# Attention and two mixtures of experts on one core: routing a batch in one piece instead of two halves

## The chip, the cores and the metric

The kernel runs on one core of a Trainium2 chip. The metric is the time of one execution on the device in microseconds (us), median over several runs; less is better. A profiled execution gives a trace of every engine: PE (TensorE, matrix products; PEld are its weight loads), DVE (VectorE), ACT (ScalarE), POOL (GpSimd), SP (SyncE, which issues most DMAs).

## What is computed

Three steps follow each other on 2 batches of 768 tokens with 8 heads of 40 (320 channels).

1. A gated linear attention: a recurrence over time with stabilised gates, per head `C = f*C + i*v k^T`, output `sigmoid(o) * (C q) / max(|n q|, 1)`. The kernel does it in chunks of 128 tokens, 6 per batch, 12 in all.
2. A mixture of 8 experts. Each token goes to the two experts with the largest noisy logits:

```python
logits = x @ w_gate
noise_scale = np.log1p(np.exp(x @ w_noise))
noisy_logits = logits + noise_scale * noise
top2 = np.argpartition(-noisy_logits, 2, axis=1)[:, :2]
top2_w = np.exp(top2_l - max); top2_w /= top2_w.sum() + 1e-09
out[mask] += top2_w[mask, k, None] * (np.maximum(x[mask] @ w1[e], 0) @ w2[e])
```

3. A dense mixture of 4 experts: every token through all four, weighted by normalised given probabilities.

Expert products are done in a split form: each fp32 operand is a high part (fp32r) and a remainder.

## The kernel before

**Attention** (lines 321 to 499, 881). Chunk `i` (0 to 11; 0 to 5 are batch 0) needs some twenty operations, each a small function `o_...`. `attn` is a generator whose every step does one of four pieces (`STEP`, lines 47 to 52) for a running index `i`: piece (i,0) has the state update U(i), the decays D of chunk i+2, the routing logits lg of chunk i-2 (L490, copied by ACT in L491); piece (i,1) has the transposes tp (L455) and the output x (L462 to L468) of chunk i-1, qg of chunk i+1 and the state product inter(i) (L440); piece (i,2) has the decay product G of chunk i+2 (L368); piece (i,3) has S of chunk i+1 (L382), AV(i) (L447), Cu(i) (L426) and the transposes xp of chunk i-1 (L478). So the logits of a batch's last chunk come in piece (7,0) for batch 0 and (13,0) for batch 1. While `alone` is set, a product is preceded by one with zeros (L344).

**Routing** (`route`, line 508; `routed_`, line 593). `route(b, h)` is a generator of ten steps on a half `h` of batch `b` (chunks 0 to 3, or 4 and 5). Step 1: Exp and Ln on ACT, two DVE operations. Step 2: the pairwise comparison `df` and its sum. Step 3: the masks `selb`, `sel`. Step 4: PE counts the tokens ahead of each token (`pp`, L537 and L541). Step 5: eleven small DVE operations on 8 values per chunk (L547 to L558). Step 6: slots and the one-hot matrix `oh` (L570), 256 values per chunk. Step 7: `in_col` and `rh` (L572 to L576). Step 8 is empty. Step 9: PE multiplies `oh` and `rh` into a table (`pt`, L581), DVE adds it; after the second half it is cast to `tok`. Step 10: `back`. `routed_` gives the mixing weights and counts. `tok` is what POOL's indirect DMAs (`xload`, L646) need to gather an expert's tokens; `prep` (L649) transposes and splits those.

**Experts.** `moe1(n)` has 8 steps per unit: four of stage 1 (L207), four of stage 2 (L221). The first four units (experts 0 to 3, batch 0) need only batch 0's routing; unit 4 needs batch 1's. Weights stream in through four `raw` buffers (`w_load`), and ACT and DVE split them (`w_split`, L187 and L188).

**The order.** Two strings set it by hand (lines 36, 37; `follow`, line 982). A group is what stands between two blanks; `A` is the next piece of attention, `r` and `q` a step of the first and the second half's routing, `F` a step of `routed_`, `w` a split of expert 0's first weights with a load, `l` a load, `g` the second sigmoid, `X` the gathers of two units, `P` the first `prep`. PLAN1 runs alone, before the experts; the line that closes `follow` (L997) takes one more piece `A`, so PLAN1 reaches (8,3). PLAN2's groups alternate with the steps of the first four units.

```python
PLAN1 = "A A A A A A A A Al A Ag Al A Al A Al Ar Ar Ar Ar Awr Ar Awr Ar qr Aqr q Aq q Aq q q A qX w A w F A P q F F"
PLAN2 = "AA AA AA AA AA AAr AAr AAr AAr Ar Ar Arq rq rq rq q q q q q q F F F"
```

In PLAN1 the first `r` stands with piece (5,1), the first `q` behind (7,0), the first half's ninth step right behind that `q`. Each engine runs its instructions in a fixed order; on PE it follows the plan.

Of the kernel before, what the change touches and what calls it, by code (L numbers as in the profile page):

```python
# [7 lines left out]
F32 = mybir.dt.float32  # L8
F32R = mybir.dt.float32r
BF16 = mybir.dt.bfloat16  # L10
# [6 lines left out]
P = 128  # L17
B, H, S, D = 2, 8, 768, 40
NC = S // P
# [3 lines left out]
E1, E2, F = 8, 4, 1024  # L23
# [3 lines left out]
NCOL = 4  # L27
# [7 lines left out]

PLAN1 = "A A A A A A A A Al A Ag Al A Al A Al Ar Ar Ar Ar Awr Ar Awr Ar qr Aqr q Aq q Aq q q A qX w A w F A P q F F"
PLAN2 = "AA AA AA AA AA AAr AAr AAr AAr Ar Ar Arq rq rq rq q q q q q q F F F"
RAW = 3 * F // NQ
# [27 lines left out]
def body(ctx: ExitStack, tc: tile.TileContext, d, o, dbg=None):  # L66
    nc = tc.nc
# [5 lines left out]
    at = at_cm.__enter__()  # L73
# [40 lines left out]
    tok = [const.tile([P, E1, NCOL], I32, name=f"tok_{b}") for b in range(B)]  # L114
# [112 lines left out]
    front = {}  # L227
# [71 lines left out]
    def sigmoid(b, after):  # L299
        with tc.issue_after(after):  # L300
            s2 = nc.scalar.activation(xs[b], xs[b], AF.Sigmoid)
        with tc.issue_after(s2.ins):
            front["table"] = nc.scalar.preload_act_table_set("natural_log_exp_and_others").ins
        return front["table"]
# [189 lines left out]
    done = set()  # L494
# [9 lines left out]

    HALVES = (slice(0, 4), slice(4, NC))
    rt = [{}, {}]

    def route(b, h):
        t = rt[b]
        if h == 0:  # L510
            nl = at.tile([P, NC, E1], F32, name="nl")
            selb = at.tile([P, NC, E1], BF16, name="selb")
            sel = at.tile([P, 2, NC, E1], F32, name="sel")
            t.update(nl=nl, selb=selb, sel=sel)
        nl, selb, sel = t["nl"], t["selb"], t["sel"]
        n = HALVES[h]
        c0, HC = n.start, n.stop - n.start
        logit = lgs[b]
        assert ("lg", b * NC + HALVES[h].stop - 1) in done
        sp = at.tile([P, HC, E1], F32, name=f"spl{h}")  # L520
        nc.scalar.activation(sp, logit[:, n, E1:], AF.Exp)
# [3 lines left out]
        yield  # L525
        df = at.tile([P, HC, E1, E1], F32, name=f"df{h}")
        nc.vector.tensor_sub(df, nl[:, n].unsqueeze(2).to_broadcast([P, HC, E1, E1]), nl[:, n].unsqueeze(3).to_broadcast([P, HC, E1, E1]))
        nc.vector.tensor_tensor(df.rearrange("p t a b -> p t (a b)"), df.rearrange("p t a b -> p t (a b)"), thr.rearrange("p a b -> p (a b)").unsqueeze(1).to_broadcast([P, HC, E1 * E1]), ALU.is_ge)
        rk = at.tile([P, HC, E1], F32, name=f"rk{h}")
        nc.vector.tensor_reduce(rk, df, AX.X, ALU.add)  # L530
# [8 lines left out]
        for i in range(1, last + 1):  # L539
            j = max(i, c0)  # L540
            nc.tensor.matmul(pp[:, j - c0 :, :], ones, selb[:, j - i : last + 1 - i, :], start=False, stop=(i == last))  # L541
        sl = at.tile([P, 3, HC, E1], F32, name=f"sl{h}")
        yield
        g = at.tile([P, HC, E1], F32, name=f"g{h}")
        spare = at.tile([P, HC, E1], F32, name=f"spare{h}")
        wide = lambda x: x.unsqueeze(1).to_broadcast([P, HC, E1])
# [12 lines left out]
        yield  # L559
        tmp = at.tile([P, 2, HC, E1], F32, name=f"tmp{h}")  # L560
        sf = at.tile([P, 3, 2, HC], F32, name=f"sf{h}")
        for w in (0, 2):
# [3 lines left out]
        K = 2 * HC  # L566
        oh = at.tile([P, K, P], BF16, name=f"oh{h}")
        rh = at.tile([P, 2, K, E1 * NCOL], BF16, name=f"rh{h}")
        in_col = at.tile([P, K, E1 * NCOL], BF16, name=f"in_col{h}")
        nc.vector.tensor_tensor(oh, count.unsqueeze(1).to_broadcast([P, K, P]), sf[:, 2].rearrange("p k c -> p (k c)").unsqueeze(2).to_broadcast([P, K, P]), ALU.is_equal)  # L570
# [12 lines left out]
        nc.vector.tensor_add(table, table, pt[:, 1])  # L583
        if h == 1:
            nc.vector.tensor_copy(tok[b].rearrange("p e j -> p (e j)"), table)
            routed.add(b)
        yield
# [310 lines left out]
    def fill(n):  # L898

        wps = psum([P, 4 * P], "warm")  # L900
        for i in range(n):
            nc.tensor.matmul(wps, zero[:, :P], zero, start=(i == 0), stop=(i == n - 1))  # L902
# [68 lines left out]
    def splits():  # L971
        for _ in range(NQ):
            with behind():
                w_split()
                w_load()
            yield
# [5 lines left out]
    def follow(plan, b, first):  # L982
        r, q, f, w = route(b, 0), route(b, 1), routed_(b), splits()
        for group in plan.split():
            for t in group:
                if t in "Arqfw":
                    next({"A": A, "r": r, "q": q, "w": w}[t], None)
                elif t == "F":
                    next(f, None)
                elif t == "X":  # L990
                    xload(first)
                    xload(first + 1)
                else:
                    {"l": behind_load, "P": lambda: prep(first), "g": lambda: sigmoid(1, front["act"])}[t]()
            yield
        for g in (A, r, q, f):
            assert next(g, None) is None or g is A  # L997
# [111 lines left out]
```

## Time and profile before

| what | value |
|---|---|
| median of 3 runs | 709.69 us (709.32 to 710.06) |
| profiled execution | 709.88 us, span of its trace 708.1 us |
| PE busy | 690.0 us, 97% of the span |
| DVE, ACT, POOL busy | 370.3, 254.7, 82.1 us |
| mean granted TensorE clock | 0.986 |
| HBM read, written | 64.07 MB, 8.92 MB |

The span is what the trace covers; 1.78 us of the execution lie around it. An engine's share is a mean over stages: attention fills the first 100 us, experts with attention go on to about 130 us, and from there on it is experts almost alone. The granted clock is 1.00 when TensorE runs at 2.4 GHz and 0.50 at 1.2 GHz.

### The profile page before, as it was taken

The numbers are of one execution on the slowest core, as the hardware profiler recorded it, in microseconds if no ns is written. First come the engines' busy times: TensorE is split into PE (matmuls) and PEld (weight loads), VectorE is DVE, ScalarE is ACT, GpSimd is POOL, SyncE is SP. The second block draws the span as 40 slices with busy tenths as digits, with TensorE's granted clock in tenths as the row PEclk, the third lists the DMA queues.
The fourth block names the chain that finished last, engine by engine and source line by source line (L and its number), as shares of the span: only waits on it lengthen the run. The fifth ranks groups of instructions, "written<-read, shape, count | busy, mean of one in ns | idle before, by whom it ended". The sixth has DMA issues, their size and how long they took to land.

```text
span 708.1 us, 11630 instructions
## 1 busy us (share of the span) xinstructions
PE 690.0 (97%) x4612; PEld 616.8 (87%) x4616; DVE 370.3 (52%) x834; ACT 254.7 (36%) x475; POOL 82.1 (12%) x143
## 2 busy tenths in 40 slices
PE   9999789999999999999899999999999999999997
PEld 4566569999999999999889899898998998989987
DVE  7857868797564655658756424412344124332131
ACT  4964236453453543545541313302233013121120
POOL 5211041005012101124024000000000000000000
PEclk9999689999999999999999999999999999999999
DMA  8345446656365454567662003100031001001011
GB/s 276 109 156 181 131 149 184 180 182 219 109 193 164 129 152 127 144 191 243 185 195 82 0 12 101 52 0 1 20 108 37 1 1 38 1 0 38 1 38 40
DMA packets 36434, 73.79 MB, mean 104 GB/s; under 512 B 7576, under 2 KB 14744, under 8 KB 36376
## 3 DMA queue, kind: packets, MB, share of 16 engines
q1 hardware_dynamic: 33752, 64.16, 29.7%
q0 software_dynamic: 2624, 8.85, 4.4%
q8 instruction: 38, 0.62, 0.4%
q14 instruction: 20, 0.16, 0.1%
HBM read 64.07 MB, written 8.92 MB: 103 GB/s over the span
## 4 chain that ended last, share of the span: by engine, by line
PE 87%; DVE 5%; DMA 3%; ACT 2%; issue 2%; POOL 0%; SPq 0%; ACTq 0%; DVEq 0%; POOLq 0%
PE z L207 25%; PE z L221 24%; PE s L207 13%; PE s L221 12%; PE sp L382 2%; PE warm L902 2%; DMA raw<-w 1%; PE s L217 1%; PE hp L440 1%; PE hp L447 1%; DMA raw<-v 1%; PE lp L490 1%; PE pa L660 1%; DVE w1lo L188 1%; PE up L414 1%
## 5 line engine op out<-in xcount | busy, mean ns | idle before, releaser
L224 ACT ACTIVATE hh<-z 128x512 fp32r<-128x512 f32 x96 | 56.9, 598 | 192.7 <-PE z L207 188.8
L221 PE MATMUL z<-w2hi,hh 128*128 128x320 f32 x384 | 118.5, 309 | 0.0
L221 PE MATMUL z<-w2hi,hl 128*128 128x320 f32 x384 | 118.3, 308 | 0.0
L221 PE MATMUL z<-w2lo,hh 128*128 128x320 f32 x384 | 118.3, 308 | 0.0
L207 PE MATMUL z<-x2h,w1hi 128*128 128x512 f32 x288 | 112.4, 390 | 0.0
L221 PE MATMUL s<-w2hi,hh 128*128 128x320 f32 x448 | 108.2, 313 | 2.0 <-ACT hh L224 1.2
L225 DVE SCALAR_TENSOR_TENSOR hl<-z,hh 128x512 fp32r<-128x512 f32 x96 | 65.8, 689 | 82.6 <-ACT hh L224 82.6
L207 PE MATMUL z<-x2h,w1lo 128*128 128x512 f32 x288 | 96.6, 389 | 0.0
L207 PE MATMUL s<-xh,w1hi 128*128 128x256 f32 (+1 forms) x288 | 84.9, 312 | 0.0
L188 DVE TENSOR_TENSOR w2lo<-raw,w2hi 128x640 fp32r<-128x640 f32 x60 | 49.1, 822 | 66.4 <-ACT w2hi L187 64.2
L221 PEld LDWEIGHTS s<-w2hi,hh 128*128 128x128 f32 x448 | 77.0, 188 | 3.1 <-ACT hh L224 1.5
L187 ACT CAST w2hi<-raw 128x640 fp32r<-128x640 f32 x60 | 43.6, 728 | 90.0 <-PE s L217 25.2
L207 PE MATMUL z<-x2l,w1hi 128*128 128x512 f32 x192 | 74.8, 390 | 0.0
L188 DVE TENSOR_TENSOR w1lo<-raw,w1hi 128x768 fp32r<-128x768 f32 x60 | 57.3, 955 | 31.6 <-ACT w1hi L187 30.9
L221 PEld LDWEIGHTS z<-w2lo,hh 128*128 128x128 f32 x384 | 72.1, 188 | 0.6
L221 PEld LDWEIGHTS z<-w2hi,hh 128*128 128x128 f32 x384 | 72.1, 188 | 0.5
L221 PEld LDWEIGHTS z<-w2hi,hl 128*128 128x128 f32 x384 | 72.1, 188 | 0.0
L207 PE MATMUL s<-xh,w1lo 128*128 128x256 f32 (+1 forms) x288 | 70.6, 309 | 0.0
L221 PE MATMUL s<-w2lo,hh 128*128 128x320 f32 x224 | 69.3, 309 | 0.0
L187 ACT CAST w1hi<-raw 128x768 fp32r<-128x768 f32 x60 | 50.1, 836 | 39.7 <-PE s L207 20.2
L207 PEld LDWEIGHTS z<-x2h,w1lo 128*128 128x128 f32 x288 | 54.1, 188 | 11.3
L207 PEld LDWEIGHTS z<-x2h,w1hi 128*128 128x128 f32 x288 | 54.0, 188 | 10.8
(208 smaller groups left out, 994.2 us busy)
## 6 DMA issues: line engine op xcount, KB each, us to landing
raw<-w SPq DMA_DIRECT2D x44, 384.0 KB
raw<-w SPq DMA_DIRECT2D x44, 320.0 KB
raw<-v SPq DMA_DIRECT2D x16, 384.0 KB
raw<-v SPq DMA_DIRECT2D x16, 320.0 KB
kv<-kv SPq DMA_DIRECT2D x12, 324.0 KB
Yd<-ys SPq DMA_DIRECT2D x8, 320.0 KB
kp<-kT SPq DMA_DIRECT2D x12, 208.0 KB
qt<-qT SPq DMA_DIRECT2D x12, 208.0 KB
```

The lines of the kernel that those rows point to most:

```text
L187: nc.scalar.copy(hi, raw)
L188: nc.vector.tensor_sub(lo, raw, hi.bitcast(F32))
L207: nc.tensor.matmul(out_ps, l, r, start=(i == 0), stop=(i == len(seq) - 1))
L217: nc.tensor.matmul(yp, both[f], r[:, k], start=(f == 0 and i == 0), stop=(f == NF - 1 and i == 1))
L221: nc.tensor.matmul(yp, l, r, start=(f == 0 and i == 0), stop=(f == NF - 1 and i == 2))
L224: nc.scalar.activation(hh, src, AF.Relu)
L225: nc.vector.scalar_tensor_tensor(hl, src, 0.0, hh.bitcast(F32), ALU.max, ALU.subtract)
L382: nc.tensor.matmul(sp[g][:, j, :], t["kp"][r, j, :], t["qt"][r, j, :], start=anew, stop=(anew or j == 3))
L414: nc.tensor.matmul(up[64 * j : 64 * j + m, p, :], t["kw"][:, h : h + m], t["kv"][:, 4 * j + p, D:], start=True, stop=True)
L440: nc.tensor.matmul(hp[64 * j : 64 * j + m, p, :], Cs[c % 2][r, 41 * p : 41 * p + m], t["qg"][r, p, :], start=(anew and p == 0), stop=False)
L447: nc.tensor.matmul(hp[64 * j : 64 * j + 41, p, :], t["kv"][:, 4 * j + p, D:], t["A"][:, 4 * j + p, :], start=False, stop=(p == 3))
L902: nc.tensor.matmul(wps, zero[:, :P], zero, start=(i == 0), stop=(i == n - 1))
```

## The change

`route` takes all six chunks of a batch at once: one set of ten steps per batch, each operation on 48 values where it was on 32 and on 16 (the larger ones in proportion). The letter `q` goes, and `o` is new: six products with zeros (`fill(6)`). Both plans are new. In PLAN1 the four `w` stand with pieces (5,1), (5,3), (6,1) and (6,3); no routing is issued before (7,0); the first step follows (7,0), steps 2 and 3 follow (7,1), step 4 follows (7,2), 5 is with (7,3), 6 with (8,0), 7 with (8,1), then 8, `o`, and 9 with `X`. PLAN1 with the closing line reaches (9,0). In PLAN2 the attention has 16 pieces in 11 groups, and the ten steps of batch 1 follow, one per group, in groups 12 to 21.

```diff
-PLAN1 = "A A A A A A A A Al A Ag Al A Al A Al Ar Ar Ar Ar Awr Ar Awr Ar qr Aqr q Aq q Aq q q A qX w A w F A P q F F"
-PLAN2 = "AA AA AA AA AA AAr AAr AAr AAr Ar Ar Arq rq rq rq q q q q q q F F F"
+PLAN1 = "A A A A A A A A Al A Ag Al A Al A Al Aw A Aw A Aw A Aw A r A rr A r Ar Ar Ar r o rX A rF A F P F"
+PLAN2 = "AA A AA A AA A AA A AA A A r r r r r r r r r r F F F"
...
-    HALVES = (slice(0, 4), slice(4, NC))
...
-    def route(b, h):
+    def route(b):
         t = rt[b]
...
-        n = HALVES[h]
-        c0, HC = n.start, n.stop - n.start
+        n, c0, HC = slice(0, NC), 0, NC
         logit = lgs[b]
-        assert ("lg", b * NC + HALVES[h].stop - 1) in done
-        sp = at.tile([P, HC, E1], F32, name=f"spl{h}")
+        assert ("lg", b * NC + NC - 1) in done
+        sp = at.tile([P, HC, E1], F32, name="spl")
...
-        if h == 1:
-            nc.vector.tensor_copy(tok[b].rearrange("p e j -> p (e j)"), table)
-            routed.add(b)
+        nc.vector.tensor_copy(tok[b].rearrange("p e j -> p (e j)"), table)
+        routed.add(b)
...
     def follow(plan, b, first):
-        r, q, f, w = route(b, 0), route(b, 1), routed_(b), splits()
+        r, f, w = route(b), routed_(b), splits()
...
-                if t in "Arqfw":
-                    next({"A": A, "r": r, "q": q, "w": w}[t], None)
+                if t in "Arw":
+                    next({"A": A, "r": r, "w": w}[t], None)
...
-                    {"l": behind_load, "P": lambda: prep(first), "g": lambda: sigmoid(1, front["act"])}[t]()
+                    {"l": behind_load, "o": lambda: fill(6), "P": lambda: prep(first), "g": lambda: sigmoid(1, front["act"])}[t]()
             yield
-        for g in (A, r, q, f):
+        for g in (A, r, f):
             assert next(g, None) is None or g is A
```

The other lines of the diff only drop the half from the names of tiles.

## Rows read from the trace of the kernel before

**Rows 1.** The page: busy time of each engine.

```profile
PE 690.0 (97%) x4612; PEld 616.8 (87%) x4616; DVE 370.3 (52%) x834; ACT 254.7 (36%) x475; POOL 82.1 (12%) x143
```

**Rows 2.** What PE waited for, 40 to 200 us: total, times, longest.

```profile
PE pt L581 <- DVE rh L576: 7.9, 3, 4.2
```

**Rows 3.** PE in order of time: start, duration, work, [idle before <-releaser].

```profile
66.78 1.16 PE L382 MATMUL sp<-qt,kp 40*128 40x128 f32 x16
...
70.91 0.84 PE L490 MATMUL lp<-wgn,xt 128*128 128x16 f32 x6
75.98 0.61 PE L581 MATMUL pt<-rh,oh 128*128 128x64 bf16 x8 [4.23 <-DVE rh L576]
...
81.66 2.08 PE L382 MATMUL sp<-qt,kp 40*128 40x128 f32 x16
...
91.24 0.29 PE L581 MATMUL pt<-rh,oh 128*128 128x64 bf16 x2 [1.87 <-DVE rh L576]
...
101.13 0.36 PE L207 MATMUL s<-xh,w1hi 128*128 128x256 f32 x1
```

**Rows 4.** Stages: length, busy PE, PEld, DVE, ACT, POOL, clock, DMA share, GB/s.

```profile
74.00:76.00 2.00, 0.02 (x1) 0.03 (x2) 2.00 (x6) 0.82 (x2) 0.00 (x0) 0.53 0.25 99
76.00:78.00 2.00, 2.00 (x17) 1.48 (x19) 2.00 (x17) 0.63 (x1) 0.00 (x0) 0.50 0.00 0
...
86.00:88.00 2.00, 1.67 (x20) 1.06 (x18) 0.50 (x4) 0.88 (x4) 0.00 (x0) 0.56 0.90 236
...
90.00:92.00 2.00, 0.76 (x7) 0.74 (x8) 2.00 (x4) 1.85 (x3) 0.50 (x1) 0.80 0.00 0
```

**Rows 5.** DVE's groups by form, 57 to 102 us: busy, mean ns, idle before.

```profile
L388 DVE TENSOR_TENSOR A<-sp,A 128x512 f32<-128x512 f32 x8 | 5.4, 683 | 0.7 <-PE sp L382 0.7
L188 DVE TENSOR_TENSOR w1lo<-raw,w1hi 128x768 fp32r<-128x768 f32 x4 | 3.8, 944 | 0.0
...
L570 DVE TENSOR_TENSOR oh<-count,sf 128x1024 bf16<-128x1024 f32 x1 | 1.2, 1214 | 0.0
...
L527 DVE TENSOR_TENSOR df<-nl 128x256 f32<-128x256 f32 x1 | 0.4, 418 | 0.0
...
L527 DVE TENSOR_TENSOR df<-nl 128x128 f32<-128x128 f32 x1 | 0.3, 277 | 0.0
...
L551 DVE TENSOR_TENSOR g<-g,cap 128x32 f32<-128x32 f32 x1 | 0.2, 179 | 0.0
...
L557 DVE TENSOR_TENSOR sl<-sl,ebase 128x16 f32<-128x16 f32 x1 | 0.2, 166 | 0.0
```

**Rows 6.** DVE in order of time, 65 to 160 us.

```profile
72.28 0.66 DVE L557 TENSOR_TENSOR sl<-sl,ebase 128x32 f32<-128x32 f32 x1
...
92.77 0.18 DVE L585 CAST tok<-table 128x32 int32<-128x32 f32 x1
...
159.61 0.68 DVE L570 TENSOR_TENSOR oh<-count,sf 128x512 bf16<-128x512 f32 x1
```

**Rows 7.** POOL in order of time, 65 to 97 us.

```profile
71.68 1.22 POOL L361 TENSOR_SCALAR_AFFINE_SELECT A<-A 128x512 f32<-128x512 f32 x2 [5.30 <-ACT A L360]
...
93.87 1.52 POOL L646 DMA_INDIRECT xe<-Xall,tok  x1 [3.37 <-DVE xo L467]
```

**Rows 8.** PE, 100 to 170 us, in order of time.

```profile
103.22 0.66 PE L414 MATMUL up<-kv,kw 128*64 128x41 f32 x16
...
104.23 0.84 PE L490 MATMUL lp<-wgn,xt 128*128 128x16 f32 x6
...
160.64 0.23 PE L581 MATMUL pt<-rh,oh 128*128 128x64 bf16 x2 [1.78 <-DVE rh L576]
```

**Rows 9.** Stages 100 to 160 us, columns as in rows 4.

```profile
100.00:110.00 10.00, 10.00 (x115) 8.76 (x114) 6.69 (x18) 4.76 (x11) 3.11 (x4) 1.00 0.96 318
...
140.00:160.00 20.00, 18.87 (x156) 18.44 (x154) 19.61 (x63) 11.18 (x19) 0.00 (x0) 1.00 0.59 180
```

More of the change, by code (lines that the diff above doesn't have):

```diff
@@ L502, in body @@
     LAST = max(-k for piece in steps for _, k in piece)
-    HALVES = (slice(0, 4), slice(4, NC))
     rt = [{}, {}]
-    def route(b, h):
+    def route(b):
         t = rt[b]
[L510 to L515, printed above, removed]
-        n = HALVES[h]
-        c0, HC = n.start, n.stop - n.start
+        nl = at.tile([P, NC, E1], F32, name="nl")
+        selb = at.tile([P, NC, E1], BF16, name="selb")
+        sel = at.tile([P, 2, NC, E1], F32, name="sel")
+        t.update(nl=nl, selb=selb, sel=sel)
+        n, c0, HC = slice(0, NC), 0, NC
         logit = lgs[b]
-        assert ("lg", b * NC + HALVES[h].stop - 1) in done
-        sp = at.tile([P, HC, E1], F32, name=f"spl{h}")
+        assert ("lg", b * NC + NC - 1) in done
+        sp = at.tile([P, HC, E1], F32, name="spl")
         nc.scalar.activation(sp, logit[:, n, E1:], AF.Exp)
@@ L525, in route @@
         yield
-        df = at.tile([P, HC, E1, E1], F32, name=f"df{h}")
+        df = at.tile([P, HC, E1, E1], F32, name=f"df")
         nc.vector.tensor_sub(df, nl[:, n].unsqueeze(2).to_broadcast([P, HC, E1, E1]), nl[:, n].unsqueeze(3).to_broadcast([P, HC, E1, E1]))
         nc.vector.tensor_tensor(df.rearrange("p t a b -> p t (a b)"), df.rearrange("p t a b -> p t (a b)"), thr.rearrange("p a b -> p (a b)").unsqueeze(1).to_broadcast([P, HC, E1 * E1]), ALU.is_ge)
-        rk = at.tile([P, HC, E1], F32, name=f"rk{h}")
+        rk = at.tile([P, HC, E1], F32, name=f"rk")
         nc.vector.tensor_reduce(rk, df, AX.X, ALU.add)
@@ L541, in route @@
             nc.tensor.matmul(pp[:, j - c0 :, :], ones, selb[:, j - i : last + 1 - i, :], start=False, stop=(i == last))
-        sl = at.tile([P, 3, HC, E1], F32, name=f"sl{h}")
+        sl = at.tile([P, 3, HC, E1], F32, name=f"sl")
         yield
-        g = at.tile([P, HC, E1], F32, name=f"g{h}")
-        spare = at.tile([P, HC, E1], F32, name=f"spare{h}")
+        g = at.tile([P, HC, E1], F32, name=f"g")
+        spare = at.tile([P, HC, E1], F32, name=f"spare")
         wide = lambda x: x.unsqueeze(1).to_broadcast([P, HC, E1])
@@ L559, in route @@
         yield
-        tmp = at.tile([P, 2, HC, E1], F32, name=f"tmp{h}")
-        sf = at.tile([P, 3, 2, HC], F32, name=f"sf{h}")
+        tmp = at.tile([P, 2, HC, E1], F32, name=f"tmp")
+        sf = at.tile([P, 3, 2, HC], F32, name=f"sf")
         for w in (0, 2):
@@ L566, in route @@
         K = 2 * HC
-        oh = at.tile([P, K, P], BF16, name=f"oh{h}")
-        rh = at.tile([P, 2, K, E1 * NCOL], BF16, name=f"rh{h}")
-        in_col = at.tile([P, K, E1 * NCOL], BF16, name=f"in_col{h}")
+        oh = at.tile([P, K, P], BF16, name=f"oh")
+        rh = at.tile([P, 2, K, E1 * NCOL], BF16, name=f"rh")
+        in_col = at.tile([P, K, E1 * NCOL], BF16, name=f"in_col")
         nc.vector.tensor_tensor(oh, count.unsqueeze(1).to_broadcast([P, K, P]), sf[:, 2].rearrange("p k c -> p (k c)").unsqueeze(2).to_broadcast([P, K, P]), ALU.is_equal)
```

## The prediction, made before the change was run

> **What bounds the kernel now.** First the page's busy times: PE is busy 690.0 us of a span of 708.1 [rows 1], so all but some 18 us is matrix work that the change leaves as it is. What can move is PE's idle time and the time that its work takes at the lower clock. The view of waits is read next: between 40 and 200 us PE waited 7.9 us, three times, for one thing, the table product `pt` of the routing, which needs `rh` from DVE [rows 2]. Two of these waits lie ahead of the experts. The first, 4.23 us, comes right after the logits of chunk 5, which end at 71.75 (70.91 + 0.84); the second is 1.87 us, at 91.24 [rows 3]. The stages around them show the rest: in the first wait the granted clock falls from 1.00 to 0.50 (2.4 to 1.2 GHz) at about 74 and comes back inside 86 to 88; the wait at 91 takes it down again [rows 4]. At the low level the 16 products `sp` take 2.08 us where they took 1.16 [rows 3]. So from 71.75 to the first expert product at 101.13 [rows 3] PE spends 29.4 us, part idle, part slow. DVE is the cause: it is busy 2.00 of 2.00 us on both sides of the first wait [rows 4], with the first half's routing, the attention and two weight splits of 0.94 us [rows 5] on it. The end of the stretch is set by `tok`: cast from 92.77 to 92.95 [rows 6], then POOL's gathers [rows 7], `prep`, and the first product 8.2 us behind `tok`.
>
> **Chunk 5's logits stay at 71.75.** Up to there PE is the bound, and the change takes only four tiny products from it. The four splits now all lie ahead of it: 2 x 0.94 us more on DVE [rows 5]. In exchange the first half's routing leaves: its steps before that point (eight operations of steps 1 to 3, most of step 5) are some 16 small ones of 0.18 and three of 0.42 [rows 5], 4.1 us. DVE gets lighter by some 2.2 us, and the backlog that made the first wait should be gone. Bounds 71.4 and 72.7 (all of a split late on the path); I take 71.75. The four loads that go with the splits are issued earlier on SP's queue, between the attention's loads; cover is the idle share of the DMA engines before 72, and without it the price is one late `kv`, under 1 us, inside the same bounds.
>
> **The routing itself.** A half has 33 operations on DVE. 25 are small: 0.166 us on 16 values, 0.179 on 32 [rows 5], so about 0.19 on 48. Three are of the kind of `df`: 0.277 on 128, 0.418 on 256 [rows 5], so 0.56 on 384. `oh` is 0.68 on 512 [rows 6] and 1.21 on 1024 [rows 5], so 1.75 on 1536. The four around `in_col`, priced like `df` by their sizes, are 0.95, 1.4 and 1.8. The halves make 6.6 + 8.4 = 15.0 us, the whole 10.0: DVE saves 5.0 us per batch. But behind 71.75 the second half had 6.6 us, and now there are 10.0.
>
> **From the logits to `pp`.** The copy, Exp and Ln on ACT take about 0.9 us, to 72.7. On DVE then come steps 1 to 3 up to `selb`: three small, three `df`, and by the plan ahead of steps 2 and 3 piece (7,1)'s `x` and `qg`. An operation's successor starts some 0.08 before it ends, so: 3 x 0.11 + 3 x 0.48 + `x` 1.3 (six operations by size) + `qg` 0.6 = 3.7. `selb` at 76.4, `pp` until 76.8. PE meanwhile has (7,1) and (7,2), some 2.3 us, to 74.0: **a new wait of 2.4 us in front of `pp`**, where the plan of before waited 4.23 for `pt`. Bounds: none if routing goes ahead of `x` and `qg`, 5.5 if everything pending goes ahead of it. Queued on PE behind the waiting `pp` are S(8) and AV(7), and behind these everything of chunk 8.
>
> **Does that wait cost the clock?** A wait of 1.87 us took it down, in the same kind of thin work [rows 3, 4]; one of 1.78 us among dense expert products [rows 8] left the stage at 1.00 [rows 9]. The first is nearer: I take it that the clock falls at about 77 and stays low as long as after the first fall, 74 to 87.7.
>
> **From `pp` to `pt`.** PE has (7,3), (8,0), (8,1) and `fill(6)`: at full clock 3.1 + 2.4 + 1.7 + 1.4 = 8.6 us, by the length of the same pieces of chunks 6 and 7 before 71.75. DVE has step 5 (11 x 0.11), steps 6 and 7 (0.5 + 1.7 + 1.4) and the attention's two products by S (0.68 each [rows 5]), `kw`, `Cu`, `x`, `qg`, 4.2 by size: 9.0. `oh` can run into POOL's two selections behind (8,0), as L557 did (0.66 us at 72.28 [rows 6] for 0.17 otherwise [rows 5], while POOL ran its pair [rows 7]): 0.5 more, 9.5. At full clock DVE is the bound: `pt` at 86.3. With the clock low (factor 1.8 by the two `sp` rows, 1.9 with the thin products around them) PE is: about 7.3 of its 8.6 us of work are done when the clock returns at 90.7, the rest by 91 to 92; I take 91.2. `pt` (12 products) and the two sums 0.8: `tok` at 92.0, the first expert product 8.2 later, **100.2**. Piece (9,0) now lies ahead of it, in the time that PE waits for gathered rows; before it was behind, 103.22 to 105.07, 1.85 us [rows 8]. The comparable start of before is 101.13 + 1.85 = 103.0. **Gain 2.8 us.** `fill(6)` is counted above; it costs nothing where DVE is the bound.
>
> The Trainium skill says in "Perfetto Trace Analysis", section "Optimizing Scalar/DVE Operations", that larger grouped operations help where the engine is saturated, while breaking them up lets work finish sooner where it isn't but causes bubbles elsewhere. DVE is saturated before 79 us, so the rows put this change under the first half of that rule; by the second half the sum would be the slower rival's, below.
>
> **Batch 1.** DVE is busy 19.61 of 20 us from 140 to 160 [rows 9], with both halves on it, and `pt` waits 1.78 us [rows 8]. The change saves 5.0 us of DVE there, but its ten steps come one per group, with `oh` among the ReLUs of unit 2. Of the wait I take 1.0 as gained; bounds a gain of 2.5 and a loss of 2.5.
>
> **Sum**, against the profiled execution (708.1 us of span and 1.78 around it): 709.88 - 2.8 - 1.0 = 706.1. The median of the runs is 0.19 lower: **705.9 us**. A measurement can tell about 0.2%, 1.4 us.
>
> **The rivals.** (1) *The clock holds*, because the wait at `pp` is short. Then `pt` is at 86.3, `tok` at 87.3, the start at 95.5 to 96: gain 7.0 instead of 2.8, **701.7**. For it: DVE is free at 72. Against: 2.4 us is longer than the 1.87 that cost the clock.
>
> (2) *Slower: one long chain behind the last logits.* Nothing is routed ahead of them any more, and the 3.4 us by which 10.0 exceeds 6.6 lie on the chain. If all pending attention work on DVE (two products by S, `kw`, `Cu`: 2.7 us, and the collision with POOL, 0.5) goes ahead of `selb`, `pp` comes at 80.0, after 5.5 us idle, and the clock stays low through the thin work that follows: 8.6 x 1.9 = 16.3, `pt` at 96.4, `tok` 97.4, start 105.6, 2.6 us behind 103.0. Batch 1 gains nothing then, for the same reason: **712.3**. It decides if `pp` comes after 79. For it: the 3.4 us and the single `pp` in front of all of chunk 8. Against: the 2.2 us taken off DVE before 72. By the second half of the Trainium skill's rule above, this is how it would go.
>
> (3) *No change: the gain is given back behind the start.* From 100 to 110 the DMA engines are busy 0.96 of the time [rows 9]; a start 3 us earlier asks for expert 1's weights earlier, at the same rate of loads. Then PE waits for weights, and batch 1's block costs what it saves: **709.5**. For it: the 0.96. Against: all four splits, and the loads behind them, come earlier too.
>
> **How the numbers follow.** Forecast 0.40 (its own range 703.8 to 708.2), clock holds 0.22, slower 0.24, no change 0.14. Faster: 0.39 + 0.22 = 0.61, less 0.02 of the third: 0.60. Same: 0.15. Slower: 0.25, with the loss of 2.5 on batch 1. The range reaches to 700.5 (the clock holds and batch 1 gives a little more) and to 712.5, which takes in the slower rival's point and leaves out its further half and the far ends, under 2 in 10.
>
> **What would show it.** Right: no wait for `pt` near 72, a wait of 2 to 3 us at `pp`, granted clock 0.50 from about 77 to 90, `tok` near 92, first expert product near 100 with (9,0) ahead of it, DVE's routing near 10 us per batch. Wrong: `pp` after 79 or the first product after 103 (rival 2), a clock of 1.00 through 77 to 87 (rival 1), waits for `raw` behind 100 us (rival 3).

## The result, and the profile after

The changed kernel takes 715.39 us (median of 20 runs, 709.3 to 719.7) where the kernel before takes 709.79 us (20 runs): a ratio of **1.0072, interval 1.0049 to 1.0096**. It is slower by 0.7%; the forecast was 705.9, with a range that ended at 712.5. Two later comparisons, on two chips, gave 1.0089 (1.0054 to 1.0123) and 1.0029 (1.0005 to 1.0052). The sign holds, the size moves.

The profiled execution took 714.45 us, its span 712.6 us, at a mean granted clock of 0.981. First the page's busy times, which answer to [rows 1]:

```profile
PE 695.1 (98%) x4616; PEld 619.3 (87%) x4616; DVE 362.9 (51%) x768; ACT 254.5 (36%) x471; POOL 83.1 (12%) x143
```

DVE got lighter, by 7.4 us and 66 instructions, as the change promises. PE got busier by 5.1 us; the sum at the end of this section puts 3.0 us of that on matrix work at the lower clock and 2.2 on added work. The waits of PE between 40 and 200 us, which answer to [rows 2], show what became of the idle time:

```profile
PE pa L655 <- DMA xe<-Xall,tok: 5.4, 2, 4.8
PE xp L478 <- DVE x L468: 2.3, 1, 2.3
PE pp L533 <- DVE selb L528: 1.4, 1, 1.4
PE pt L577 <- DVE rh L572: 0.4, 1, 0.4
```

Two more lines of that view before the change, for comparison:

```profile
PE xp L478 <- DVE x L468: 0.7, 1, 0.7
PE pa L660 <- DMA xe<-Xall,tok: 0.5, 1, 0.5
```

The waits for `pt` have shrunk from 7.9 us to 0.4. In their place the wait for the gathered rows (`pa`, the first transposes of `prep`) has grown from 0.5 us to 5.4 and that for the transposes of batch 1's last chunk (`xp`) from 0.7 to 2.3, and 1.4 us for `pp` are new. PE in order of time, 70 to 112 us, against [rows 3]:

```profile
71.11 0.84 PE L490 MATMUL lp<-wgn,xt 128*128 128x16 f32 x6
...
76.59 0.18 PE L533 MATMUL pp<-selb,tri 128*128 128x48 bf16 x1 [1.41 <-DVE selb L528]
...
82.05 1.46 PE L490 MATMUL lp<-wgn,xt 128*128 128x16 f32 x6
...
86.55 2.34 PE L897 MATMUL warm<-zero 128*128 128x512 bf16 x6
...
89.83 0.35 PE L577 MATMUL pt<-rh,oh 128*128 128x64 bf16 x6
...
92.65 0.27 PE L479 MATMUL xp<-ident,x 128*64 128x128 f32 x1
97.76 0.66 PE L655 MATMUL pa<-ident,xe 128*128 128x128 f32 x2 [4.84 <-DMA xe<-Xall,tok]
...
99.83 0.69 PE L655 MATMUL pa<-ident,xe 128*128 128x128 f32 x2 [0.61 <-DMA xe<-Xall,tok]
...
101.25 1.03 PE L344 MATMUL dp<-zero 128*128 128x512 bf16 x2
102.21 0.79 PE L358 MATMUL dp<-tq,tk 32*128 32x512 f32 x2
102.93 1.46 PE L490 MATMUL lp<-wgn,xt 128*128 128x16 f32 x6
104.23 0.56 PE L207 MATMUL s<-xh,w1hi 128*128 128x256 f32 x1
```

Up to 92.9 us all went as forecast or better. Then PE has nothing left and stands for 4.84 us until the first rows arrive. Piece (9,0) comes after that wait, on both sides of the second `pa`, and its logits take 1.46 us there, as at 82.05, where they take 0.84 at full clock [rows 8]. The first expert product starts at 104.23; before it started at 101.13 [rows 3]. The stages show the clock (columns as in rows 4: length, busy PE, PEld, DVE, ACT, POOL, clock, DMA share, GB/s):

```profile
74.00:78.00 4.00, 2.59 (x37) 1.90 (x38) 4.00 (x14) 2.43 (x4) 0.00 (x0) 1.00 0.47 148
78.00:82.00 4.00, 4.00 (x31) 2.09 (x28) 3.36 (x16) 0.97 (x3) 0.00 (x0) 0.51 0.74 213
...
88.00:90.00 2.00, 2.00 (x26) 1.14 (x24) 1.91 (x9) 0.06 (x1) 0.00 (x0) 0.91 0.00 0
...
94.00:96.00 2.00, 0.00 (x0) 0.00 (x0) 1.92 (x6) 0.00 (x0) 1.54 (x2) 0.80 0.76 195
96.00:98.00 2.00, 0.24 (x2) 0.27 (x2) 0.00 (x0) 0.00 (x0) 1.54 (x2) 0.50 0.92 228
...
104.00:106.00 2.00, 2.00 (x10) 2.00 (x11) 0.02 (x1) 0.29 (x2) 1.11 (x2) 0.50 0.65 178
106.00:108.00 2.00, 2.00 (x12) 2.00 (x10) 0.00 (x0) 0.00 (x0) 0.00 (x0) 0.50 0.13 50
```

The granted clock falls to 0.50 (1.2 GHz) at 78 and is back by 90. In the bare wait it falls again, and now the expert products run at that level too, up to 108.75 us by a finer cut of the same view. Before, the second fall ended at 98, ahead of the experts. Note the DMA share as well: 0.76 to 0.92 while the gathers run, where before it was 0.00 at 90 to 92 [rows 4], and to 96 by the same view.

In batch 1 a wait of 2.29 us, 0.71 before, and a fall of the clock, 1.00 before [rows 9], stand at the transposes of the last chunk; PE in order of time, and the stages there:

```profile
140.16 0.28 PE L207 MATMUL s<-xh,w1lo 128*128 128x256 f32 x1
142.73 0.46 PE L478 MATMUL xp<-ident,x 128*128 128x128 f32 x2 [2.29 <-DVE x L468]
```

```profile
142.00:144.00 2.00, 1.27 (x7) 1.30 (x8) 1.19 (x3) 0.51 (x2) 0.00 (x0) 0.74 0.61 136
144.00:146.00 2.00, 2.00 (x12) 2.00 (x11) 0.00 (x0) 0.02 (x1) 0.00 (x0) 0.50 0.50 181
```

**Where the time went.** Cut into stretches of 1 to 5 us, the stages give a sum: the span is PE's idle time, plus the time lost at the low clock (busy time times one minus the granted clock, added up), plus the rest, which is PE's work at full clock.

| us | before | after | difference |
|---|---|---|---|
| span | 708.1 | 712.6 | +4.5 |
| idle | 18.1 | 17.5 | -0.6 |
| lost at the low clock | 9.1 | 12.1 | +3.0 |
| of that 70 to 92 / 92 to 112 / 130 to 170 us | 6.1 / 3.0 / 0.0 | 5.1 / 5.2 / 1.7 | -1.0 / +2.2 / +1.7 |
| work at full clock | 680.9 | 683.1 | +2.2 |

So the idle time that the change takes from `pt` is idle again elsewhere, the low clock costs 3.0 us more, and PE has 2.2 us more work. Among it are the six zero products and two more with zeros inside (9,0) (101.25 in the view above).

### The profile page after: what moved, and what is told of

Its sections match the earlier page's. It is cut to its first block, busy times and chain, and to the rows that moved or that the text cites. A ratio compares the mean times of both kernels' runs of the same rounds, so it can differ in the third digit from the quotient of the medians.

```text
span 712.6 us, 11566 instructions
## 1 busy us (share of the span) xinstructions
PE 695.1 (98%) x4616; PEld 619.3 (87%) x4616; DVE 362.9 (51%) x768; ACT 254.5 (36%) x471; POOL 83.1 (12%) x143
## 4 chain that ended last, share of the span: by engine, by line
PE 76%; DVE 2%; issue 0%; ACT 0%; DVEq 0%; ACTq 0%
PE z L207 24%; PE z L221 24%; PE s L207 13%; PE s L221 11%; PE s L217 1%; PE pa L655 1%; DVE hh L225 0%; PE pb L656 0%; PE xq L768 0%; DVE w1lo L188 0%; ACT w1hi L187 0%; DVE oh L566 0%; DVE w2lo L188 0%; PE xq L769 0%; DVE ys L729 0%
## 5 line engine op out<-in xcount | busy, mean ns | idle before, releaser
L221 PE MATMUL z<-w2hi,hh 128*128 128x320 f32 x384 | 118.6, 309 | 0.0
L221 PE MATMUL z<-w2hi,hl 128*128 128x320 f32 x384 | 118.3, 308 | 0.0
L221 PE MATMUL z<-w2lo,hh 128*128 128x320 f32 x384 | 118.3, 308 | 0.0
L221 PE MATMUL s<-w2hi,hh 128*128 128x320 f32 x448 | 108.4, 313 | 1.3 <-DVE hh L225 1.3
L207 PE MATMUL s<-xh,w1hi 128*128 128x256 f32 (+1 forms) x288 | 86.9, 318 | 0.0
L221 PEld LDWEIGHTS s<-w2hi,hh 128*128 128x128 f32 x448 | 76.8, 188 | 2.6 <-DVE hh L225 1.8
L187 ACT CAST w2hi<-raw 128x640 fp32r<-128x640 f32 x60 | 43.6, 728 | 92.9 <-PE s L217 23.9
L221 PEld LDWEIGHTS z<-w2lo,hh 128*128 128x128 f32 x384 | 72.1, 188 | 0.6
L221 PEld LDWEIGHTS z<-w2hi,hh 128*128 128x128 f32 x384 | 72.1, 188 | 0.5
L221 PEld LDWEIGHTS z<-w2hi,hl 128*128 128x128 f32 x384 | 72.1, 188 | 0.0
L221 PE MATMUL s<-w2lo,hh 128*128 128x320 f32 x224 | 69.2, 309 | 0.0
```

The source lines that it names most:

```text
L187: nc.scalar.copy(hi, raw)
L207: nc.tensor.matmul(out_ps, l, r, start=(i == 0), stop=(i == len(seq) - 1))
L221: nc.tensor.matmul(yp, l, r, start=(f == 0 and i == 0), stop=(f == NF - 1 and i == 2))
```

## The experiments

Ratios are medians to the kernel before on the same chip, with 95% intervals. The first four ran on one chip, the next four on a second, then four on a third, and three pairs on three more. Parts are set against each other within a chip where a pair allows it; the changed kernel itself ran beside runs 5 to 7 (as run 8) and beside run 17 (as run 18), not beside the others.

**1. Zeros in the bare wait.** Twenty zero products ahead of the first `prep` (a new letter G, `fill(20)`).

```diff
-... r o rX A rF A F P F"
+... r o rX A rF A F G P F"
```

> The kernel after, with 20 products of zeros (some 4.4 us at the full clock) on PE right ahead of the first prep, where PE waited 4.84 us for the gathered rows. Theory A (the wait for gathered rows, bare of PE work, takes the clock down a second time, and prep, piece (9,0) and the first expert products run at 1.2 GHz): granted clock 1.00 from 90 to 110, first expert product 2 us earlier, the time 3 to 5 us below the kernel after, 710.5 to 712.5. Theory B (the longer routing chain itself is the loss): no more than 1 us below, 714.5 to 716. Theory C (the loss is in batch 1's part, behind 130 us): as B.

Measured: 713.93 us, 1.0036 (1.0008 to 1.0064). The clock held at `pp` in this profile, stood at 1.00 to 97.75, and fell just behind a wait of 2.15 us for the second tile; the first expert product came at 100.75. The zeros are 4.48 us of PE time, most of it in time that was idle, and the ratio lies among the changed kernel's own three. In this run filling the wait was no repair: the zeros don't bring the rows, the wait for the second tile is bare, and (9,0) stands behind it as before.

**2. Zeros in front of `pp`** (S is `fill(8)`).

```diff
-... A r A rr A r Ar ...
+... A r A rr A S r Ar ...
```

> The kernel after, with 8 products of zeros (some 1.8 us) on PE ahead of pp, where PE waited 1.41 us and the clock fell. Theory A': the first fall is what stretches the pieces up to pt; without it pt comes at 86 to 87 instead of 89.8 (DVE is then the bound), tok 3 us earlier, and the time is 2 to 4 us below the kernel after, 711.5 to 713.5; the wait for gathered rows stays. Theory B: DVE sets pt either way; pt within 1 us of 89.8 and the time 714.5 to 716.

Measured: 712.07 us, 1.0025 (1.0001 to 1.0048). The clock holds through 86, and PE is early: `pt` then waits 2.06 us, in which the clock falls (low from 88.25 to 105.25), and the gathers 3.57 us. With the clock kept through the middle of the chain, the fall came at the next wait.

**3 and 4. One batch at a time.** Batch 0 whole with the new PLAN1 and batch 1 in halves with the old PLAN2; and the reverse (there PLAN2's last three groups of attention are AA, AA, A, since the old PLAN1 leaves one piece more).

```diff
-        r, f, w = route(b), routed_(b), splits()
+        r, q, f, w = route(b, 2 if b == 0 else 0), iter(()) if b == 0 else route(b, 1), routed_(b), splits()
```

(`HALVES` has a third entry, `slice(0, NC)`, and the whole batch shares its tiles with the second half; for the reverse `b == 1` stands in both places.)

> Batch 0 routed whole with the plan of the kernel after, batch 1 in halves with PLAN2 of the kernel before. Theories A and B (the loss lies ahead of the experts): most of the 5.6 us loss stays, 713 to 715.5. Theory C (batch 1): it goes, 709.5 to 711.5.

> Batch 0 in halves with PLAN1 of the kernel before, batch 1 whole with PLAN2 of the kernel after (one more piece of attention in its first groups, since PLAN1 of before reaches one piece less). Theories A and B: 709 to 711.5, near the kernel before. Theory C: 713 to 715.5, with a wait of PE of over 2 us near 140.

Measured: batch 0 alone 711.02 us, 1.0002 (0.9978 to 1.0025); batch 1 alone 710.65 us, 1.0012 (0.9990 to 1.0035). Neither part by itself differs from the kernel before by more than the measurement tells. Batch 1 alone shows its wait:

```profile
PE xp L478 <- DVE x L468: 2.2, 1, 2.2
```

and the clock at 0.50 in the 2 us behind it, although batch 0 is as before. That wait belongs to the second plan, not to the late start of the experts.

**5. Piece (9,0) ahead of the first `prep`.** Nothing else moves.

```diff
-... r o rX A rF A F P F"
+... r o rX A rF A F A P F"
...
-        for g in (A, r, f):
+        for g in (r, f):
-            assert next(g, None) is None or g is A
+            assert next(g, None) is None
```

> The kernel after with piece (9,0) put ahead of the first prep instead of behind it, so that its products (2.4 us at the full clock, 3.6 at the low one) run while PE waits for gathered rows. Theory A (the wait for gathered rows is bare and what stands between prep and the first expert product is run at 1.2 GHz): the first expert product comes 2.1 to 2.5 us behind the second gather's transposes instead of 4.4, PE's idle time there falls by some 2 us, and the time is 2 to 4 us below the kernel after. Theory B (the length of the routing chain alone): within 1 us of the kernel after.

Measured: 711.86 us, 1.0019 (0.9996 to 1.0042), on a chip where the changed kernel itself gave 716.37 us, 1.0089 (run 8): 4.5 us less for one letter moved. In this profile PE does not wait for the rows: (9,0)'s logits end at 95.85 (94.39 + 1.46), and the first transposes run at once. PE in order of time:

```profile
95.69 0.67 PE L655 MATMUL pa<-ident,xe 128*128 128x128 f32 x2
...
96.36 0.63 PE L655 MATMUL pa<-ident,xe 128*128 128x128 f32 x2
...
97.73 0.58 PE L207 MATMUL s<-xh,w1hi 128*128 128x256 f32 x1 [0.52 <-ACT xh L199]
```

From the second `pa` to the first expert product it takes 1.4 us; in the changed kernel 4.4. This is the order that the prediction had assumed of the changed kernel. The 4.5 us are not all the order's, though. The clock held at `pp` here, ahead of the place where the order differs, and the executions' mean granted clock is 0.988 where run 8 has 0.983. And only one product comes so early: some 2.7 us of piece (9,1) stand between it and the second one, at 100.84. A fairer mark is the first product of stage 2 (L221), ahead of which the same work lies in either order. Here are two pairs of profiles that differ in the place of (9,0) alone, each pair with the same clock behind `pp` but on two chips: run 5 and run 18 (clock held), then run 12 and run 13 (clock fell).

```profile
116.85 0.39 PE L221 MATMUL s<-w2hi,hh 128*128 128x320 f32 x1
119.21 0.39 PE L221 MATMUL s<-w2hi,hh 128*128 128x320 f32 x1
```

```profile
123.00 0.39 PE L221 MATMUL s<-w2hi,hh 128*128 128x320 f32 x1
125.64 0.39 PE L221 MATMUL s<-w2hi,hh 128*128 128x320 f32 x1
```

With (9,0) first (the upper line of each pair), PE is 2.4 and 2.6 us earlier there. That is what the traces show of the order alone, at that place. With batch 1 in halves the same mark comes only 0.2 and 0.5 us earlier (run 9 at 121.04, runs 3 and 17 at 121.24 and 121.54): there run 17's wait for the rows was shorter, 1.9 us, and run 3's clock had held to 94.75.

**6. Before, with zeros in its two waits.** G is `fill(16)`, S `fill(8)`.

```diff
-... Awr Ar qr Aqr q Aq q Aq q q A qX w ...
+... Awr Ar qGr Aqr q Aq q Aq q q A SqX w ...
```

> The kernel before with products of zeros in its two waits for pt: 16 (3.5 us) ahead of the first and 8 (1.8 us) ahead of the second. If PE's clock is what the waits cost (theory A), the clock stays at 1.00 from 70 to 100, some 9 us lost to it go, and the first expert product comes 3 to 6 us earlier, 704 to 707 us. If the chain of DVE, POOL and DMA sets the start whatever PE's clock (theory B), the zeros only add to PE's work where they miss the wait: 709 to 712 us.

Measured: 711.24 us, 1.0010 (0.9988 to 1.0031). The profile has the clock at 1.00 from 78 to 98, and then 5.4 us of waiting for the gathers; the first expert product comes at 104.45, later than the 101.13 of [rows 3]. But the profile is no clean test of the start, for in it the clock had already fallen, from 68.5 to 75.5, ahead of the zeros of G at 76.66 and behind a wait that the profile before does not have:

```profile
67.16 0.58 PE L455 MATMUL tp<-ident,hs 105*128 105x105 f32 x4 [0.95 <-DVE A L388]
```

Chunk 5's logits end at 76.81 there instead of 71.75, and `tok` still comes 0.5 us earlier, at 92.42: behind the logits the chain took 5.6 us less (15.6 instead of 21.2). PE then waited for the gathers, and in the median nothing was gained.

**7. Before, with the four splits at the new places.**

```diff
-... Al Ar Ar Ar Ar Awr Ar Awr Ar qr Aqr q Aq q Aq q q A qX w A w F A P q F F"
+... Al Awr Ar Awr Ar Awr Ar Awr Ar qr Aqr q Aq q Aq q q A qX A F A P q F F"
```

> The kernel before (halves) with only the four weight splits moved to where the kernel after has them. If the new place of the splits, not the joining of the halves, is what moves the time (theory D): DVE is fuller before 72, the first wait for pt grows from 4.2 to some 6 us, and the time is 2 to 4 us above before. If it is the joining (A, B): within 1.5 us of before.

Measured: 715.42 us (6 runs), 1.0082 (1.0053 to 1.0111). In the halves, early splits cost as much as the whole change does: `pt` waits 9.6 us instead of 7.9, and the clock is down from 90 to 107. Two other splits (of `w2`, at 85.09 and 90.36) move up into the gap and stand in front of the second `oh`, at 91.09, on DVE. So the early place of the splits is a rival for part of the loss; with the whole routing, run 10 is its only test.

**8. The changed kernel again**, on the chip of runs 5 to 7.

> The kernel after once more, beside the other runs of this call. Its span should again split into PE's work at the full clock (683 us), PE's idle time (17 to 18) and the time lost to the low clock (8 to 13, changing from execution to execution), 712 to 716 us in all.

Measured: 716.37 us, 1.0089 (1.0054 to 1.0123); the wait for the gathers is 5.02 us there.

**9. Piece (9,0) first, and batch 1 in halves.** The edits of 5 and 3 together.

> Batch 0 whole with (9,0) ahead of the first prep, batch 1 in halves with PLAN2 of before: the two edits that each took some 4.5 us off the kernel after, together. If they act in different places (the wait for gathered rows; the wait for xp near 140), they add: 705 to 708.5, below the kernel before. If both gains are the same thing (the clock that an execution happens to have at 75 to 110), 710 to 712.

Measured: 708.95 us, 0.9984 (0.9968 to 1.0001). With its order mended, routing batch 0 whole is at least no slower than the halves; it just misses the 705 to 708.5 of the expectation.

**10. The last two splits behind the gathers.**

```diff
-... Al Aw A Aw A Aw A Aw A r A rr A r Ar Ar Ar r o rX A rF A F P F"
+... Al A A A A Aw A Aw A r A rr A r Ar Ar Ar r o rX w A w rF A F P F"
```

> The kernel after with the last two weight splits put back behind X, where the kernel before has them. Theory D (the early place of the splits is the loss, as in the run with halves): 709.5 to 712. Theory A (bare wait for gathered rows and (9,0) behind prep): 714 to 717, within 1.5 us of the kernel after.

(The four splits keep their sequence, so the first two move to (6,1) and (6,3).) Measured: 712.90 us, 1.0050 (1.0028 to 1.0073), between the two expectations. DVE's relief by itself brought nothing in this profile: the gathers start at 92.23, 0.55 us earlier than in the changed kernel, but the wait for their rows is 5.77 us, the longest of all. With the splits their loads moved beside the gathers. The stages (columns as above):

```profile
92.00:94.00 2.00, 0.96 (x13) 0.57 (x9) 2.00 (x7) 0.75 (x3) 1.47 (x2) 1.00 1.01 362
94.00:96.00 2.00, 0.00 (x0) 0.00 (x0) 1.62 (x5) 1.27 (x4) 1.70 (x2) 0.82 1.09 386
```

From the first gather's start to the first `pa` it takes 6.49 us (92.23 to 98.72) at 362 and 386 GB/s; in the changed kernel 4.98 (92.78 to 97.76) at 237 and 195 GB/s; before at most 3.74 (93.87 to 97.61), with the DMA engines idle to 96. More loads beside the gathers, later rows, in these three; but no run moved the loads alone, and run 7 does not fit: its rows took 3.51 us (94.70 to 98.21) beside 184 GB/s on the mean.

**11. Without the six zero products** (`o` taken out of PLAN1).

> The kernel after without its six products of zeros ahead of pt. If they are mere work on PE, the engine that bounds the kernel, the time falls by 1.3 us: 713.5 to 715. If they hold the clock up or fill a wait for pt that is there anyway, it stays or rises: 715 to 718, with a longer wait for pt.

Measured: 712.19 us, 1.0027 (1.0012 to 1.0042). PE's work falls by 1.4 us in the sum above (683.1 to 681.7), and `pt` waits 1.0 us in two pieces. The clock fell at `pp` here as in the profile above, so the two can be set side by side: `pt` comes 0.7 us earlier (89.12) and the first expert product 0.6 (103.61). Of the 1.4 us of zeros, then, some 0.6 lie on the path. The time does not show it: with the zeros the ratios were 1.0029, 1.0072 and 1.0089, but in other comparisons.

**12. Piece (9,0) first, and a new rhythm for batch 1.** The single groups of PLAN2 stand together behind the double ones.

```diff
-PLAN2 = "AA A AA A AA A AA A AA A A r r ...
+PLAN2 = "AA AA AA AA AA A A A A A A r r ...
```

> The kernel after with (9,0) ahead of the first prep, and with PLAN2's sixteen pieces in another rhythm (five groups of two, then six single ones), so that two groups instead of one lie between the output x of chunk 11 and its transposes xp, where PE waited 2.3 us near 140 and the clock fell. If that wait is the loss of batch 1: it falls under 1 us, the clock stays at 1.00 there, and the time is 2 to 3 us below the run with (9,0) first alone, 708.5 to 710. If it only moves on: 711 to 713.

Measured: 707.30 us, **0.9949 (0.9922 to 0.9976)**. The wait for `x` is gone and the clock stays at 1.00 through 140 to 146. Taken alone, this looked like a version that beats both; run 15 put that right.

**13. The new rhythm alone.** The order of (9,0) is left as the change has it.

> The whole routing with the second plan's rhythm alone altered: its single groups stand together behind the double ones, so that batch 1's last logits get two groups of expert work between x and xp. Theory (batch 1 is a term of its own): the wait for x near 142 us (2.29 us) and the stretch at 1.2 GHz behind it (1.7 us of loss) both go, the start of the experts stays as it is with a gather wait near 4.8 us; ratio to the kernel before 1.001 to 1.004, where the whole routing has 1.007. Rival (the second plan gave its gain only together with the earlier start, or by chance of the clock): ratio 1.006 to 1.009, with the wait gone or not.

Measured: 710.88 us, 1.0011 (0.9985 to 1.0038), as the theory had it. The first expert product comes at 103.62, nearly as late as in the changed kernel, and the gathers' wait is 4.47 us; what is gone is batch 1's wait. The stages at that place:

```profile
142.00:144.00 2.00, 2.00 (x20) 2.00 (x19) 1.60 (x4) 1.50 (x5) 0.00 (x0) 1.00 0.78 232
144.00:146.00 2.00, 2.00 (x20) 2.00 (x19) 1.78 (x4) 1.18 (x5) 0.00 (x0) 1.00 0.78 253
```

**14. Run 12 without the zeros.**

> Piece (9,0) ahead of the first prep, the second plan's altered rhythm, and the six zero products of 128x512 behind pp left out. Theory (the zeros are PE work on the path): PE's work falls by 1.3 us, a wait for rh of about 1 us comes back in front of the table products, so 0.5 to 1.5 us less than with the zeros: ratio 0.992 to 0.995. Rival (the zeros keep the clock up where DVE is the bound, and pay for themselves): the clock falls again at the table products, 1 to 3 us more than with the zeros: ratio 0.996 to 0.999.

Measured: 711.45 us, 1.0014 (0.9994 to 1.0034), outside both expectations. PE now waits 3.03 us for `rh` and the clock falls there, at 88.

**15 and 16. Runs 12 and 14 side by side** on one more chip.

> The mended plan once more ((9,0) ahead of the first prep, second plan's altered rhythm, six zero products behind pp). Theory (its gain is that of the two orders, on any chip): ratio 0.993 to 0.998. Rival (0.9949 was the chip): ratio 0.999 to 1.003.

> The mended plan without the six zero products, on the same chip as the kernel with them. Theory (in this order DVE is the bound up to the table products, so the zeros hide, and without them PE waits for rh, at the price of the clock): 0.3 to 0.7% slower than the mended plan with the zeros on this chip, ratio 0.999 to 1.003. Rival (the zeros are 1.3 us of work on the path in any order, and the run without them fell on a slower chip): 0.1 to 0.3% faster than with them.

Measured: with the zeros 710.12 us, 1.0005 (0.9983 to 1.0027); without 710.42 us, 1.0008 (0.9987 to 1.0029). In the mended order the zeros neither cost nor save anything that the measurement tells. And the 0.9949 does not hold on this chip. Its interval speaks for one chip, and between comparisons on two chips the same kernel moved by 0.6%. The mended plan is not shown to beat the kernel before.

**17 and 18. Batch 0 whole and both whole, side by side**, on the last chip.

> Batch 0 whole with the new first plan, batch 1 in halves with the old second plan, on the same chip as the whole routing. Theory (batch 1's part is a term of its own, a wait of 2.3 us and 1.7 us of low clock, and most of what the change loses): 0.5 to 0.8% faster than the whole routing on this chip, ratio to the kernel before 0.999 to 1.003. Rival (the parts were set apart by their chips): within 0.3% of the whole routing on this chip.

> The changed kernel a third time, the partner of the run above. Theory: ratio 1.006 to 1.010, as in its first two comparisons. Rival (its loss hangs on the chip as the mended plan's gain does): ratio below 1.004.

Measured: batch 0 whole 709.69 us, 1.0006 (0.9985 to 1.0028); both 711.58 us, 1.0029 (1.0005 to 1.0052). Batch 1's part is 1.9 us, 0.27%: inside the 0.3% of the rival and short of the theory's 0.5%, and 1.0029 is under the 1.004 of the other rival. The intervals overlap. The waits of the second, and its stages at the two falls:

```profile
PE pa L655 <- DMA xe<-Xall,tok: 3.9, 1, 3.9
PE pt L577 <- DVE rh L572: 2.3, 2, 1.9
PE xp L478 <- DVE x L468: 2.3, 1, 2.3
PE pp L533 <- DVE selb L528: 1.4, 1, 1.4
```

```profile
78.00:82.00 4.00, 4.00 (x48) 2.80 (x48) 3.69 (x21) 1.91 (x5) 0.00 (x1) 1.00 0.82 252
...
94.00:96.00 2.00, 1.12 (x8) 0.77 (x9) 0.00 (x0) 0.00 (x0) 1.16 (x2) 0.50 1.07 278
```

This is the same program as the one above. The same 1.4 us in front of `pp` leave the clock at 1.00 here; the first expert product comes 3.4 us earlier, at 100.78. Yet the span is 713.0 us, 0.4 longer: behind batch 1's wait the low clock, down from 141 to 148, costs 3.4 us where it cost 1.7, and another 1.6 us is lost to it between 300 and 400 us.

## Why the prediction was wrong

DVE in order of time, for the steps on the routing (against [rows 5, 6]):

```profile
73.56 0.55 DVE L523 TENSOR_TENSOR df<-nl 128x384 f32<-128x384 f32 x1
...
76.64 0.81 DVE L188 TENSOR_TENSOR w2lo<-raw,w2hi 128x640 fp32r<-128x640 f32 x1
...
85.78 1.75 DVE L566 TENSOR_TENSOR oh<-count,sf 128x1536 bf16<-128x1536 f32 x1
...
91.68 0.18 DVE L580 CAST tok<-table 128x32 int32<-128x32 f32 x1
```

By the prediction's own steps:

- **Chunk 5's logits at 71.75**: 71.95 (71.11 + 0.84). Right.
- **DVE's price of the routing, 10.0 us a batch**: right. `df` was to take 0.56, `oh` 1.75, and all its operations' durations come to 20.6 us for the two batches. The saving was less: the page's busy time fell by 7.4 us, not by twice 5.0. What was missed are two splits of `w2` that stand in the chain (76.64 is the first), work that moved up into the gap; with the clock down, PE was later still, so they did not set `pt`.
- **The wait in front of `pp`, 2.4 us, and `pp` until 76.8**: 1.41 us, and `pp` at 76.59. The mechanism was right, and so was the time; the wait was shorter because AV(7), 1.08 us at 74.10, ran ahead of `pp` on PE.
- **The clock falls at 77 and is back at 90.7**: in this profile 78.0 to 88.25. Right here, but with some luck: in other executions it held, see the last section.
- **`pt` at 91.2 and `tok` at 92.0**: 89.83 and 91.86. That `tok` came on time is luck: `pt` came 1.4 us early, and from it to `tok` it took 2.0 us where the sum had 0.8. (The sum's own terms, the clock back at 90.7 and 1.3 us of work left, make 92.0 for `pt` and not the 91.2 that it took.)
- **"The first expert product 8.2 later, 100.2. Piece (9,0) now lies ahead of it, in the time that PE waits for gathered rows"**: this is **the step that failed**. From `tok` to the product it took 12.4 us (91.86 to 104.23). The 8.2 were read off a kernel in which PE had work during the gathers and 2.1 us of it between the second tile's transposes and the product. Here PE's last work ends at 92.92; the plan names P before the closing A, so (9,0) is issued behind the first `pa` and can't start in the wait. So the wait is bare, the clock falls in it, and (9,0) and the first unit run at 1.2 GHz, up to 108.75; the prediction had put this second fall at nothing. The 4.2 us by which 12.4 exceed 8.2 have two parts. The distance from the second `pa` to the product is 4.4 us instead of 2.1 (99.04, the kernel before's second `pa`, to 101.13). And the second gather's rows come 7.05 us behind the first gather's start (92.78 to 99.83) where they took 5.2; why they came later stays open. Run 5, with (9,0) where the prediction had put it, gives 4.5 us back on one chip, and the intervals (0.9996 to 1.0042, and 1.0054 to 1.0123) don't meet; between profiles of like clock the order is worth 2.4 and 2.6 us. These show the part that is the place of (9,0).
- **Batch 1, a gain of 1.0 with bounds of 2.5 either way**: the wait for `pt` went, as forecast. The step looked only at the ten routing steps and not at the groups of attention that PLAN2 rearranged: AA A leaves one group between the product of `x` and its transposes, in which DVE has two splits and a ReLU part ahead of the last step of `x`. A wait of 2.29 us, 0.71 before, and 1.7 us lost at the low clock, against the wait of 1.78 [rows 8] that went: a loss of 1.5 us, inside the bounds. Runs 4 and 13 show where it comes from: the wait comes with the plan alone and goes with its rhythm alone.
- **"`fill(6)` costs nothing where DVE is the bound"**: with the clock down PE was the bound up to `pt`, as the prediction's own next step said, and then the zeros are work, 1.4 us of which some 0.6 lie on the path (run 11).

In the profiled execution these terms nearly add up. The first expert product at 104.23 is 1.2 us behind the prediction's comparable 103.0, where a gain of 2.8 was forecast; the low clock from the product to 108.75 takes 2.3 us; batch 1 loses 1.5. That is 5.0 us, and the execution was 4.6 us longer than that of the kernel before.

Of the rivals, none came as it was told. (2), the slower one, had the sign and 712.3 us, and one of its two signs came, a first product after 103; but its mechanism was `pp` after 79, and `pp` came at 76.59. (1), the clock that holds, came true at `pp` in other executions, and without its gain: PE gets to `pt` early, waits there and the clock falls then. (3) had weights late; PE's waits show none for weights.

The Trainium skill says in "Perfetto Trace Analysis", section "Optimizing Scalar/DVE Operations", which the prediction weighed, that grouping operations can improve throughput where the engine is saturated. This case's trace agrees for DVE alone: its busy time fell by 7.4 us. The second half of that rule, on breaking operations up, did not decide the time: `tok`, DVE's result, came 1.1 us earlier than in the kernel before (91.86 and 92.95), and the time was lost behind it, by the order on PE.

What stays open: how the parts add up over the medians. Batch 0's part measured nothing by itself (1.0002, 1.0006), batch 1's 0.1 to 0.3%, both together 0.3 to 0.9%. Run 5 brought back 0.7% on its chip. Of the other repairs there are only ratios to the kernel before (run 13 1.0011; both repairs 0.9949 and 1.0005), to be held against the changed kernel's 1.0029 to 1.0089 of other comparisons. Between chips, and with falls of the clock that come and go, 18 runs don't settle it to 0.3%. Whether the loads beside the gathers delay them was argued from three kernels, with run 7 against it, and not shown by moving the loads alone. How much of the loss the early place of the splits makes, which alone cost the halves 0.8% (run 7), is open too.

## What to carry to other kernels

When a chain gets shorter on one engine, ask what the next engine does in the time that is won: here PE ran out of work and waited for a transfer that took no less time than before, so the saved idle time came back a few microseconds later. A duration taken from the old trace from one event to another ("8.2 us from `tok`") holds only if the work between them, and its place in the order, is the same; read the order of issue behind the wait, piece by piece, before counting work as hidden. And when a plan is made anew for one reason, cost its other rearrangements too: a group less between a result and its reader cost 1.5 us, more than the 1.0 us that the change was to gain in that batch.

## What the runs showed of the hardware

**The same wait takes the clock down or not.** In 15 profiles with batch 0 routed whole and no zeros there, PE waits 1.4 us in front of `pp`. In six of them the granted clock is 0.50 between 79 and 82 us, in nine 1.00; the changed kernel alone shows both, in the two fences of 78 to 82 above. What differs is not the wait but when it comes: in the nine `pp` starts between 75.64 and 76.38 us, in the six between 76.59 and 77.02. Why that goes with the fall no run shows. The wait of 2.3 us in batch 1 left the clock at 1.00 in run 10 and took it down in the changed kernel's three profiles and in four others (runs 1, 2, 5 and 11), where its place in time does not sort them (140.42 in run 10, 137.67 to 143.35 in the seven). So a fall that one profile shows is no fixed term of a sum: a shift of some 0.2 us in the start of the same wait can be all that tells a profile with it from one without.

**The clock carries the spread.** The 20 runs of the changed kernel go from 709.3 us at a mean granted clock of 0.991 to 719.7 us at 0.978. The difference of the clocks times the span, 0.013 x 712, is 9.3 of the 10.4 us, and over all 20 the time and the clock correlate at -0.87.

**Zeros set into PE's waits gave no version faster than the kernel before** (runs 1, 2, 6: 1.0036, 1.0025, 1.0010). Run 2's clock did hold behind `pp` at 76.83, a time at which it fell in the profiles without zeros; in its profile and in that of run 1 PE then waited for DVE's `rh` (2.06 and 1.62 us) and for the rows, and in that of run 6 for the rows.
